# Moving gates, softmax factors and weight conversions to other places in an attention pipeline's pairs

## The chip, the cores and the metric

The kernel runs on one core of one Trainium2 chip. The metric is the device time of one execution in microseconds, lower is better. The kernel before has a median of 579.82 us over three runs (577.78 to 580.89). The core's engines are named as the profile names them: PE is TensorE (PEld its weight loads), DVE is VectorE, ACT is ScalarE, POOL is GpSimd, and SP issues most of the DMAs. Each of them works through its own queue in order.

## The reference

Three blocks follow one another on 4 batches of 448 positions.

```python
# 1. attention, 12 heads of 64
scores = cap * tanh(scale * q @ k.T / cap)
x = softmax(scores) @ v                     # heads side by side: 4 x 448 x 768
# 2. four attention experts of width 64, the best 2 of 4 per position
logits = x @ w_gate                         # rank them, softmax over the best two
for e in range(4):
    a = causal_softmax((x @ wq[e]) @ (x @ wk[e]).T / 8)
    out += gate[e] * (a @ (x @ wv[e]) @ wo[e])
# 3. gated MLP on that output
h = gelu(x @ w_in); u, v = split(h)
v = layer_norm(v) * g_ln
out = x + (u * (w_sg @ v + b_sg)) @ w_out
```

All tensors are float32. The two large weights `w_in` and `w_out` arrive as float64 and are turned into pairs of float32 parts on the chip.

## The kernel before

**The pairs.** `slot(n)` (line 252) is one step of the attention. There are 24 pairs of heads (4 batches with 6 pairs each), and slots 0 to 24. In slot n, PE makes the scores of pair n in two halves (`scores`, 191), ACT takes tanh and exp of them, and PE multiplies the weights of pair n - 1 with its values (`values`, 218). DVE and POOL sum the exponentials (POOL the first sum `pb`, DVE the next two in `add_up`, 213), and after every second pair PE folds these sums over the partitions (`sums`, 229) into `rs`.

**The places.** Between these steps `slot` calls `side(place)`, at which the second block and the weights' preparation are woven in. The places of a slot come in this order: "a" (called a0) in the first half of the scores, before their exp; "w" before the values product; "a" again (a1) after it; "p" after the second half of the scores; then sums and `add_up`; "n" last. Up to slot 9 `side` comes from `prepare_weights` (559), which converts `w_in`; from slot 10 on it comes from `beside` (522). PE, ACT, DVE and POOL keep the order of the program through slot 24 (`InOrder`, `pin`), so an instruction that waits holds everything behind it on its engine. After slot 24 a scheduler chooses the order (`pe_pin[0] = False`, 642).

**Normalising.** When batch b's pairs are done, `normed` (317) does the rest in steps: `invert` (241) takes the reciprocal of `rs`, writes it to DRAM (`rd`) and loads it back spread over partitions (`rb`, two tiles, tags rb0 and rb1, `load_rb`); `over_sums` multiplies (`os`); `in_parts` splits x into `xh` and `xl` for products in parts. A batch has three such thirds, 0 to 2. The steps stand at the second, fourth and fifth slot after its last pair.

**Experts.** `PLAN` (474) lists the second block of a batch by slots counted from the one in which its x is ready: queries and keys (`queries_keys`, 355), scores with their row minima (`weigh`, 416: a PE product into a PSUM tile `a`, on DVE the masked minimum `m`, on ACT the exp `pe`, which frees the PSUM tile), values and logits (`values_chunk`, 374), the gates (`gates`, 390: 13 small DVE instructions with one ACT exp among them), the factors and POOL's scaling (`settle`, 436: six small DVE instructions for `cs`, eight on POOL that scale `pe`), transposes (`turn`, 447: PE `tr`, DVE `pt`) and the product with the values (`attend`, 459). The PSUM tiles of `weigh`, `values_chunk`, `queries_keys`, `turn` and `sums` share one pool of three buffers (`ps_g`, 124). Slots n with n % 6 = 0 (12, 18, 24) have minima and two value chunks.

**w_out.** `w_out(k, i)` (338) converts one of eight pieces of the last weight: a DMA into `wuw`, six DVE instructions (`from64`, into `wum`), three on POOL, two DMAs to DRAM (`wud`). Its tiles take the tags rb0 and rb1. Six pieces run at place "w" of slots 11, 12, 17, 18, 23 and 24, loaded one slot earlier at "n"; the other two run in `experts_end` (546), which holds all of the experts' work behind slot 24.

**The end.** After slot 24, `experts_end` is interleaved with the MLP's parts (line 827), 0.35 units of the MLP for each unit of the experts. `mlp_weights(1)` (667, 685) waits until all eight pieces of w_out are done, then loads them as `wu_h` and `wu_l`, whose buffers are those of the query and key weights. `mlp_a(1)` takes the tags rb0 and rb1 for its own `yh` and `yl` (815).

Of the kernel before, what the change touches and what calls it, by code (L numbers as in the profile page):

```python
# [13 lines left out]
I32 = mybir.dt.int32  # L14
# [58 lines left out]
def build(ctx: ExitStack, tc: tile.TileContext, a: dict):  # L73
# [48 lines left out]
    wp = ES(tc.tile_pool(name="wp", bufs=2))  # L122
    dr = ES(tc.tile_pool(name="dr", bufs=2, space=bass.MemoryType.DRAM))
# [193 lines left out]
    def normed(n, place):  # L317

        b = (n - 1) // HP - 1
        step = (n % HP, place)  # L320
        if n > B * HP + 4 or b < 0:
            return
        if step == (1, "w"):
            invert(b)
        elif step == (3, "w"):
            over_sums(b, 0)
            over_sums(b, 1)
            load_rb(b, 2)
        elif step == (4, "w"):
            in_parts(b, 0)  # L330
            in_parts(b, 1)
            over_sums(b, 2)
        elif step == (4, "a1"):
            in_parts(b, 2)
# [3 lines left out]
    def w_out(k, i):  # L338

        o = slice(i * DM // 2, (i + 1) * DM // 2)  # L340
        w = xp.tile([128, DM], F32R, tag="rb0", name=f"wuw{k}_{i}")
        me = xp.tile([128, DM], I32, tag="rb1", name=f"wum{k}_{i}")
        hi, lo = w[:, :DM // 2], w[:, DM // 2:]
        nc.sync.dma_start(w.bitcast(I64), a["w_out"][:, k, o])
        yield WC
        p, e = from64(w, me[:, :DM // 2], me[:, DM // 2:])
        rnd("p", hi, p)
        pool_e.tensor_tensor(p, p, hi.bitcast(F32), op=ALU.subtract)
        pool_e.tensor_tensor(lo, p, e, op=ALU.add)
        for t in range(2):  # L350
            nc.sync.dma_start(wu_d[t][:, k, o], (hi, lo)[t].bitcast(F32))
        wu_done.append((k, i))
        yield 1.0
# [105 lines left out]
    def attend(b, ep):  # L459
# [7 lines left out]
        if ep == 0:  # L467
# [9 lines left out]
            3: [("a", weigh, 0, 2), ("a", weigh, 0, 3), ("p", values_chunk, 2), ("p", values_chunk, 3)],  # L477
            4: [("w", gates), ("w", settle, 0), ("p", queries_keys, 1, 0), ("t", turn, 0, 0)],
# [3 lines left out]
            8: [("w", settle, 1), ("t", turn, 1, 0)],  # L482
# [3 lines left out]
    def planned(n):  # L486

        work = {"a": [], "w": [], "p": [], "t": []}
        for b in reversed(range(B)):
            for place, f, *args in PLAN.get(n - (b + 1) * HP - 4, []):  # L490
                work[place].append((b, f, args))
        return work
# [27 lines left out]
    ws = [w_out(k, i) for k in range(4) for i in range(2)]  # L520

    def beside(n):
# [4 lines left out]
        def side(place):  # L527
            if place == "a":
                drain(run(work["a"][:1]))
                del work["a"][:1]  # L530
                normed(n, halves.pop(0))
            elif place == "p":
                drain(together(run(work["p"]), run(work["t"]), 0.3))
            elif place == "w":
                drain(run(work["w"]))
                normed(n, place)
                experts_weights(n, place)
                if n > HP + 4 and n % HP in (5, 0):
                    drain(ws.pop(0))
            else:  # L540
                experts_weights(n, place)
                if n > HP + 3 and n % HP in (4, 5):
                    next(ws[0])
        return side

    def experts_end(n):

        for m in range(n, B * HP + 20):
            work = planned(m)
            for place in "aw":  # L550
                yield from run(work[place])
            normed(m, "w")
            normed(m, "a1")
            yield from together(run(work["p"]), run(work["t"]), 0.3)
            if ws:
                yield from ws.pop(0)


    def prepare_weights(pool):
# [36 lines left out]
        def side(n):  # L596
            todo = list(turns[n])

            def at_place(place):
# [16 lines left out]
                if n > 0:  # L616
                    normed(n, place)
# [5 lines left out]
    xp = ES(tc.tile_pool(name="xp", bufs=1, reuse_waits="tile"))  # L623
# [202 lines left out]
    elif ORD == 3:  # L826
        drain(together(ex, mlp(((mlp_a, 0), (mlp_weights, 1), (mlp_b, 0), (mlp_a, 1), (mlp_c, 0), (mlp_b, 1), (mlp_a, 2))), LRATIO))
# [69 lines left out]
```

## Time and profile before

| | |
|---|---|
| median of 3 runs | 579.82 us (577.78 to 580.89) |
| the profiled execution, its own time | 579.84 us |
| span of the core in it | 578.1 us |
| PE busy | 536.1 us (93%) |
| DVE busy | 375.5 us (65%) |
| ACT busy | 324.5 us (56%) |
| POOL busy | 140.8 us (24%) |
| share of the chain of waits on PE / DVE / ACT / DMA | 60% / 19% / 8% / 6% |
| mean granted PE clock | 0.973 of full |

The profile's times are from the span's start. The execution's time is 1.74 us above the span. In the chain of waits one follows back from the last instruction what released what. The tables of stretches give for each stretch the busy time of each engine and, as PEclk, the clock that PE was granted: 1.00 is 2.4 GHz, 0.50 would be 1.2 GHz throughout. In timelines a bracket gives how long the engine sat idle before the row and what released it. All instructions that go through a helper have the line of the helper (L104, L119), so one goes by tile names.

### The profile page before, as it was taken

The page shows a single profiled execution, that of the slowest core. Times are in us where ns is not written, and L with a number is a line of the kernel's source. Part 1 is how long each engine was busy: PE and PEld are TensorE (multiplying, and loading weights), DVE is VectorE, ACT ScalarE, POOL GpSimd, SP SyncE. Part 2 cuts the span into 40 slices and gives each one's busy share as a digit, 9 for nine tenths or more (in the row PEclk, how much of TensorE's full clock was granted, in tenths as well). Part 3 has the DMA queues.
Part 4 walks back from the last instruction along what each step waited for, and adds up shares of the span by engine and source line. Part 5 has one row for each costly group of instructions (what it writes and reads, how often), then busy time and mean ns, then how long its engine had stood idle before and what let it go on. Part 6 is the DMA issues. An engine that isn't in the chain of part 4 may idle for free.

```text
span 578.1 us, 7562 instructions
## 1 busy us (share of the span) xinstructions
PE 536.1 (93%) x2732; PEld 350.7 (61%) x2732; DVE 375.5 (65%) x725; ACT 324.5 (56%) x508; POOL 140.8 (24%) x180
## 2 busy tenths in 40 slices
PE   7999999798879997999968995899999999999997
PEld 2333333445545556555535763777878888989996
DVE  3999999774666754666765654857861688475310
ACT  5988888576757784767742343462643444243211
POOL 0000131133141144141163145417512121031000
PEclk9999999899999997999998999899999998999999
DMA  8974425833412231411118313100511000101111
GB/s 243 330 228 128 163 76 156 248 104 108 114 62 80 76 119 61 124 53 49 28 55 236 100 56 75 42 14 1 182 70 65 1 1 27 38 16 49 49 48 64
DMA packets 30596, 53.97 MB, mean 93 GB/s; under 512 B 3872, under 2 KB 22880, under 8 KB 30560
## 3 DMA queue, kind: packets, MB, share of 16 engines
q1 hardware_dynamic: 29408, 48.26, 27.5%
q0 software_dynamic: 1152, 5.24, 2.7%
q8 instruction: 21, 0.34, 0.3%
q14 instruction: 15, 0.12, 0.1%
HBM read 41.83 MB, written 11.67 MB: 93 GB/s over the span
## 4 chain that ended last, share of the span: by engine, by line
PE 60%; DVE 19%; ACT 8%; DMA 6%; issue 4%; POOL 2%; SPq 0%; DVEq 0%; POOLq 0%; ACTq 0%
PE o L119 15%; PE sp L119 7%; PE s L119 6%; PE qk L119 6%; PE po L119 6%; ACT p L104 5%; PE v L119 4%; DVE pb L104 3%; PE tr L454 3%; PE hu L119 3%; PE a L119 2%; DVE rs L104 2%; PE hv L119 2%; DVE wum L104 2%; PE w2ps L119 2%
## 5 line engine op out<-in xcount | busy, mean ns | idle before, releaser
L104 ACT ACTIVATE p<-s,tsc 112x896 f32<-112x896 f32 x96 | 91.3, 1004 | 25.0 <-PE s L119 20.0
L104 POOL TENSOR_TENSOR pb<-p 112x896 f32<-112x896 f32 x18 | 39.8, 2214 | 219.1 <-ACT p L104 134.8
L119 PE MATMUL s<-qp,kp 64*112 64x448 f32 x384 | 84.4, 557 | 3.5 <-ACT p L104 3.5
L104 ACT ACTIVATE p<-p,capt 112x1792 f32<-112x1792 f32 x48 | 85.9, 1790 | 1.3
L119 PE MATMUL po<-p,vv 112*64 112x448 f32 x384 | 77.3, 545 | 0.0
L104 DVE TENSOR_TENSOR pb<-pb,p 112x896 f32<-112x896 f32 x48 | 54.7, 1140 | 13.0 <-ACT p L104 12.2
L119 PEld LDWEIGHTS s<-qp,kp 64*112 64x112 f32 x384 | 31.0, 173 | 51.1 <-issue 22.4
L104 ACT ACTIVATE pe<-a,m 112x112 f32<-112x112 f32 (+3 forms) x64 | 31.1, 491 | 43.6 <-DVE m L104 41.5
L119 PEld LDWEIGHTS po<-p,vv 112*64 112x64 f32 x384 | 25.5, 136 | 45.0 <-issue 43.3
L119 PE MATMUL qk<-xh,wqk_h 128*128 128x448 f32 x96 | 39.4, 411 | 9.7 <-DVE xh L104 8.7
L454 PE MATMUL tr<-ident,pe 112*112 112x112 f32 x160 | 26.2, 276 | 12.6 <-ACT pe L104 8.2
L104 POOL TENSOR_SCALAR pe<-pe,cs 112x112 f32<-112x112 f32 (+1 forms) x64 | 32.8, 533 | 20.0 <-DVE cs L104 19.9
L119 PE MATMUL qk<-xh,wqk_l 128*128 128x448 f32 x96 | 36.1, 376 | 0.0
L119 PE MATMUL o<-gl,wu_h 128*128 128x448 f32 x96 | 35.6, 371 | 0.0
L119 PE MATMUL o<-gh,wu_l 128*128 128x448 f32 x96 | 35.3, 370 | 0.0
L119 PE MATMUL o<-gh,wu_h 128*128 128x448 f32 x96 | 35.3, 368 | 0.0
L104 DVE CUSTOM_DVE_ANT_0 a<-a,neg 112x112 f32<-112x112 f32 (+3 forms) x64 | 27.7, 466 | 10.9 <-PE a L119 10.9
L119 PE MATMUL v<-wvg_h,xh 128*112 128x260 f32 x96 | 30.7, 319 | 4.3 <-ACT pe L104 4.3
L104 DVE COPY pt<-tr 112x112 f32<-112x112 f32 (+3 forms) x32 | 14.1, 449 | 27.0 <-PE tr L454 26.9
L119 PE MATMUL a<-qk 64*112 64x112 f32 (+3 forms) x128 | 27.6, 430 | 3.7 <-ACT pe L104 2.6
L119 PEld LDWEIGHTS qk<-xh,wqk_h 128*128 128x128 f32 x96 | 18.8, 196 | 19.8 <-DVE xh L104 9.8
L454 PEld LDWEIGHTS tr<-ident,pe 112*112 112x112 f32 x160 | 19.0, 139 | 18.2 <-POOL pe L104 10.0
(226 smaller groups left out, 1132.1 us busy)
## 6 DMA issues: line engine op xcount, KB each, us to landing
kp<-in_kT_dram SPq DMA_DIRECT2D x24, 224.0 KB, 4.5
qp<-in_qT_dram SPq DMA_DIRECT2D x24, 224.0 KB, 4.6
vv<-in_v_dram SPq DMA_DIRECT2D x24, 224.0 KB, 4.4
rb<-rd SPq DMA_DIRECT2D x24, 224.0 KB, 5.0
out_dram<-ob SPq DMA_DIRECT2D x24, 224.0 KB, 1.9
wuw<-in_w_out_dram SPq DMA_DIRECT2D x8, 384.0 KB, 3.3
wud<-wuw SPq DMA_DIRECT2D x16, 192.0 KB, 1.8
ws<-in_wqk_dram SPq DMA_DIRECT2D x4, 384.0 KB, 5.8
```

Source lines behind the costliest of these rows:

```text
L104: ins = f(*args, **kw)
L119: pin(nc.tensor.matmul(*args, **kw))
L454: pin(nc.tensor.transpose(g[:CP, j * CP:(j + 1) * CP], pe[:, j * CP:(j + 1) * CP], ident))
```

## The change

Pieces of work change their places; none is added or taken away. In the pairs: the gates go from "w" of the fifth slot of a plan to "n" of the fourth; `settle` goes from "w" to a0 (a new list "s"), behind the minima of that place; the reciprocal of the sums goes from "w" to a1, behind the minima; the split of x for batches 1 to 3 has one third at "w" and two at a1 (before: two and one), and batch 0 has its first two thirds split in slot 9, the tenth pair, and the last at "w" of slot 10. In slots with n % 6 = 0 the first value chunk runs without transposes between. The conversions of w_out run at slots 11, 14, 17, 20 and 23 and, for the last three pieces, at steps 29 to 31 of `experts_end`; four of them take the tag ws. The pool `xp` is opened earlier in the program. In the MLP's order `mlp_b(0)` comes ahead of `mlp_weights(1)`.

```diff
-        if step == (1, "w"):
+        if step == (1, "a1"):
             invert(b)
         elif step == (3, "w"):
             over_sums(b, 0)
             over_sums(b, 1)
             load_rb(b, 2)
-        elif step == (4, "w"):
+        elif b == 0 and step == (3, "a1"):
             in_parts(b, 0)
             in_parts(b, 1)
+        elif step == (4, "w"):
+            if b:
+                in_parts(b, 0)
             over_sums(b, 2)
-        elif step == (4, "a1"):
+            if not b:
+                in_parts(b, 2)
+        elif b and step == (4, "a1"):
+            in_parts(b, 1)
             in_parts(b, 2)
...
-            3: [..., ("p", values_chunk, 2), ("p", values_chunk, 3)],
-            4: [("w", gates), ("w", settle, 0), ("p", queries_keys, 1, 0), ("t", turn, 0, 0)],
+            3: [..., ("p", values_chunk, 2), ("p", values_chunk, 3), ("n", gates)],
+            4: [("s", settle, 0), ("p", queries_keys, 1, 0), ("t", turn, 0, 0)],
...
-            8: [("w", settle, 1), ("t", turn, 1, 0)],
+            8: [("s", settle, 1), ("t", turn, 1, 0)],
...
-    ws = [w_out(k, i) for k in range(4) for i in range(2)]
+    W_OUT = {11: ("w", xp, "rb0", "rb1"), 14: ("n", at, "ws", "ws"), 17: ("w", at, "ws", "ws"),
+             20: ("n", at, "ws", "ws"), 23: ("w", at, "ws", "ws"),
+             29: ("n", xp, "rb0", "rb1"), 30: ("n", xp, "rb0", "rb1"), 31: ("n", xp, "rb0", "rb1")}
+    ws = {n: w_out(*divmod(u, 2), *W_OUT[n][1:]) for u, n in enumerate(W_OUT)}
...
             if place == "a":
                 drain(run(work["a"][:1]))
                 del work["a"][:1]
-                normed(n, halves.pop(0))
+                half = halves.pop(0)
+                drain(run(work.pop("s", [])))
+                normed(n, half)
             elif place == "p":
-                drain(together(run(work["p"]), run(work["t"]), 0.3))
-            elif place == "w":
-                drain(run(work["w"]))
+                first = work["p"][:1] if n % HP == 0 else []
+                drain(run(first))
+                drain(together(run(work["p"][len(first):]), run(work["t"]), 0.3))
+            else:
+                drain(run(work[place]))
                 normed(n, place)
                 experts_weights(n, place)
-                if n > HP + 4 and n % HP in (5, 0):
-                    drain(ws.pop(0))
-            else:
-                experts_weights(n, place)
-                if n > HP + 3 and n % HP in (4, 5):
-                    next(ws[0])
+                if n in W_OUT and W_OUT[n][0] == place:
+                    drain(ws[n])
+                if place == "n" and n + 1 in W_OUT:
+                    next(ws[n + 1])
...
-        drain(together(ex, mlp(((mlp_a, 0), (mlp_weights, 1), (mlp_b, 0), (mlp_a, 1), ...
+        drain(together(ex, mlp(((mlp_a, 0), (mlp_b, 0), (mlp_weights, 1), (mlp_a, 1), ...
```

## Rows read from the trace of the kernel before

**Rows 1.** The page: the span, and busy time of PE with its share.

```profile
span 578.1 us, 7562 instructions
PE 536.1 (93%) x2732; PEld 350.7 (61%) x2732; DVE 375.5 (65%) x725; ACT 324.5 (56%) x508; POOL 140.8 (24%) x180
```

**Rows 2.** Stretches, slots 10, 12, 13, 14, 18, 24: length, busy PE PEld DVE ACT POOL, PEclk.

```profile
99.34:117.01 17.67, 14.38 (x60) 7.02 (x59) 12.92 (x13) 10.35 (x11) 2.76 (x1) 0.82 0.77 230
...
127.52:142.02 14.50, 12.75 (x86) 7.59 (x85) 7.77 (x17) 9.64 (x17) 5.93 (x5) 1.00 0.44 140
142.02:156.28 14.26, 12.65 (x81) 7.51 (x77) 10.47 (x15) 10.22 (x18) 2.10 (x1) 1.00 0.23 71
156.28:171.94 15.66, 12.71 (x69) 6.59 (x68) 8.83 (x26) 10.70 (x13) 5.91 (x9) 1.00 0.36 104
...
208.77:229.27 20.50, 16.55 (x95) 11.16 (x95) 11.30 (x28) 10.99 (x19) 9.27 (x12) 0.83 0.33 105
...
295.23:312.14 16.91, 12.76 (x79) 8.95 (x79) 9.70 (x28) 3.06 (x11) 8.24 (x13) 0.80 0.42 120
...
340.00:370.00 30.00, 21.59 (x102) 15.45 (x100) 18.66 (x47) 10.84 (x30) 13.93 (x19) 0.89 0.24 56
```

**Rows 3.** Waits of PE: us in total, times, longest.

```profile
PE qk L119 <- DVE xh L104: 8.7, 3, 5.4
PE tr L454 <- ACT pe L104: 8.2, 3, 4.1
PE v L119 <- ACT pe L104: 4.3, 3, 1.7
```

**Rows 4.** Timeline of DVE in slot 18: start, us, instruction.

```profile
214.07 0.36 DVE L104 TENSOR_SCALAR wum<-wuw 128x384 int32<-128x384 int32 x1 [1.12 <-DMA wuw<-in_w_out_dram]
...
219.26 0.39 DVE L104 CUSTOM_DVE_ANT_0 a<-a,neg 112x224 f32<-112x224 f32 x1
```

**Rows 5.** Timeline of POOL in slot 18.

```profile
216.42 4.71 POOL L104 TENSOR_SCALAR pe<-pe,cs 112x112 f32<-112x112 f32 x8
```

**Rows 6.** Timeline of DVE in slot 15: the first copies of the transposes.

```profile
179.29 0.58 DVE L104 COPY pt<-tr 112x112 f32<-112x112 f32 x2 [2.43 <-PE tr L454]
```

**Rows 7.** Timeline of DVE in slot 14: `pb` of pair 13, then the gates.

```profile
158.77 2.21 DVE L104 TENSOR_TENSOR pb<-pb,p 112x896 f32<-112x896 f32 x2
...
162.13 0.17 DVE L104 TENSOR_TENSOR wt<-lg,gmx 112x16 f32<-112x16 f32 x1
```

**Rows 8.** Timeline of ACT in slot 14.

```profile
158.55 1.91 ACT L104 ACTIVATE p<-s,tsc 112x896 f32<-112x896 f32 x2
160.48 1.79 ACT L104 ACTIVATE p<-p,capt 112x1792 f32<-112x1792 f32 x1
```

**Rows 9.** Timeline of PE in slot 14: the second half of the scores.

```profile
161.13 1.76 PE L119 MATMUL s<-qp,kp 64*112 64x448 f32 x8
```

**Rows 10.** Timeline of DVE in slots 9 and 10.

```profile
101.42 2.20 DVE L104 TENSOR_TENSOR pb<-pb,p 112x896 f32<-112x896 f32 x2
...
109.77 0.96 DVE L104 TENSOR_TENSOR wvg_l<-ws,wvg_h 128x780 fp32r<-128x780 f32 x1
110.65 0.62 DVE L104 CAST xh<-os 128x896 fp32r<-128x896 f32 x1
```

**Rows 11.** Timeline of DVE in slot 16, beside a `pb` of POOL.

```profile
189.10 2.98 DVE L104 TENSOR_TENSOR os<-os,rb 128x896 f32<-128x896 f32 x1
```

**Rows 12.** Timeline of SP behind slot 24.

```profile
326.65 0.35 SPq L344 DMA_DIRECT2D wuw<-in_w_out_dram  x1
...
343.40 0.33 SPq L344 DMA_DIRECT2D wuw<-in_w_out_dram  x1
350.42 2.47 SPq L351 DMA_DIRECT2D wud<-wuw  x2
354.55 1.24 SPq L301 DMA_DIRECT2D rb<-rd  x2
```

**Rows 13.** Chain of waits, start and us: first products of `mlp_a(1)`.

```profile
404.69 2.79 PE hv L119 x12
```

More of the change, by code (lines that the diff above doesn't have):

```diff
@@ L122, in build @@
     wp = ES(tc.tile_pool(name="wp", bufs=2))
+    xp = ES(tc.tile_pool(name="xp", bufs=1, reuse_waits="tile"))
     dr = ES(tc.tile_pool(name="dr", bufs=2, space=bass.MemoryType.DRAM))
@@ L328, in normed, with w_out @@
             load_rb(b, 2)
-        elif step == (4, "w"):
+        elif b == 0 and step == (3, "a1"):
             in_parts(b, 0)
             in_parts(b, 1)
+        elif step == (4, "w"):
+            if b:
+                in_parts(b, 0)
             over_sums(b, 2)
-        elif step == (4, "a1"):
+            if not b:
+                in_parts(b, 2)
+        elif b and step == (4, "a1"):
+            in_parts(b, 1)
             in_parts(b, 2)
     wu_done = []
-    def w_out(k, i):
+    def w_out(k, i, pool, *tags):
         o = slice(i * DM // 2, (i + 1) * DM // 2)
-        w = xp.tile([128, DM], F32R, tag="rb0", name=f"wuw{k}_{i}")
-        me = xp.tile([128, DM], I32, tag="rb1", name=f"wum{k}_{i}")
+        w = pool.tile([128, DM], F32R, tag=tags[0], name=f"wuw{k}_{i}")
+        me = pool.tile([128, DM], I32, tag=tags[1], name=f"wum{k}_{i}")
         hi, lo = w[:, :DM // 2], w[:, DM // 2:]
@@ L476, in build @@
             2: [("a", weigh, 0, 0), ("a", weigh, 0, 1), ("p", values_chunk, 0), ("p", values_chunk, 1)],
-            3: [("a", weigh, 0, 2), ("a", weigh, 0, 3), ("p", values_chunk, 2), ("p", values_chunk, 3)],
-            4: [("w", gates), ("w", settle, 0), ("p", queries_keys, 1, 0), ("t", turn, 0, 0)],
+            3: [("a", weigh, 0, 2), ("a", weigh, 0, 3), ("p", values_chunk, 2), ("p", values_chunk, 3), ("n", gates)],
+            4: [("s", settle, 0), ("p", queries_keys, 1, 0), ("t", turn, 0, 0)],
             5: [("p", queries_keys, 1, 1), ("t", turn, 0, 1)],
@@ L486, in planned @@
     def planned(n):
-        work = {"a": [], "w": [], "p": [], "t": []}
+        work = {"a": [], "s": [], "w": [], "p": [], "t": [], "n": []}
         for b in reversed(range(B)):
@@ L549, in experts_end @@
             work = planned(m)
-            for place in "aw":
+            for place in "asw":
                 yield from run(work[place])
-            normed(m, "w")
-            normed(m, "a1")
+            for place in ("w", "a1"):
+                normed(m, place)
             yield from together(run(work["p"]), run(work["t"]), 0.3)
-            if ws:
-                yield from ws.pop(0)
+            yield from run(work["n"])
+            normed(m, "n")
+            if m in W_OUT:
+                yield from ws[m]
     def prepare_weights(pool):
@@ L596, in side @@
         def side(n):
-            todo = list(turns[n])
+            todo, halves = list(turns[n]), ["a0", "a1"]
             def at_place(place):
@@ L616, in at_place @@
                 if n > 0:
-                    normed(n, place)
+                    normed(n, halves.pop(0) if place == "a" else place)
             return at_place
@@ L621, in build @@
     PRE_SLOTS = HP + 4
-    xp = ES(tc.tile_pool(name="xp", bufs=1, reuse_waits="tile"))
     with tc.tile_pool(name="pre", bufs=2) as pre:
@@ L826, in build @@
     elif ORD == 3:
-        drain(together(ex, mlp(((mlp_a, 0), (mlp_weights, 1), (mlp_b, 0), (mlp_a, 1), (mlp_c, 0), (mlp_b, 1), (mlp_a, 2))), LRATIO))
+        drain(together(ex, mlp(((mlp_a, 0), (mlp_b, 0), (mlp_weights, 1), (mlp_a, 1), (mlp_c, 0), (mlp_b, 1), (mlp_a, 2))), LRATIO))
         drain(together(mlp_c(1), mlp(((mlp_b, 2), (mlp_a, 3))), L1 * 18600. / C))
```

## The prediction

> **What bounds the kernel now.** I read the page first: PE is busy 536.1 of 578.1 us [rows 1], so no change of places can save more than the other 42 us, plus what PE loses while its clock is low. DVE, the next, has 65%. So the question is where PE stands still, and the table of stretches by slot answers it [rows 2]. A stretch loses its length less PE's busy time, and its length times what PEclk lacks to 1.00, since at the lower level (1.2 instead of 2.4 GHz) a matmul takes twice as long. That gives: slot 10, 17.67 - 14.38 = 3.3 idle and 0.18 x 17.67 = 3.2 by the clock, 6.5 in all; slot 12, 1.75; slot 13, 1.6; slot 14, 2.95; slot 18, 3.95 + 0.17 x 20.5 = 7.4; slot 24, 4.15 + 0.20 x 16.91 = 7.5; and 340 to 370, 8.4 + 0.11 x 30 = 11.7. Together 39 us. The other slots show 0.9 at most and are not touched below unless said.
>
> The waits of PE say for what it stood still [rows 3]. "tr <- ACT pe" (8.2, slots 18 and 24) and "v <- ACT pe" (4.3) are no data that PE reads: the product needs a PSUM buffer, and the three are held by scores whose minimum DVE has not taken. DVE's timeline of slot 18 shows why [rows 4]. Behind the first minima stands a piece of w_out; it first waits for its DMA, starts at 214.07, and the second minimum runs at 219.26, 5.2 us later. In slot 13 the reciprocal stands in the same place. Slot 14 waits for the factors `cs`, slot 10 and 340 to 370 for `xh` ("qk <- DVE xh", 8.7 with one of 5.4).
>
> **The change part by part.** The sum is made against the profiled execution, 579.84 us with 1.74 of it outside the span; the median, 579.82, is the same.
>
> *w_out out of slots 12, 18 and 24.* The minima then follow PE at once and free the buffers. Slot 12 gives back 1.75. Slot 18 gives back 7.4, its low clock included, for the clock fell behind that wait; but the first value chunk now runs alone, and the transposes after it take its buffer, which ACT empties behind an exp of 1.79 [rows 8]. I take 1.0 for that (0 to 1.8): 6.4. In slot 24 there are no scores, so ACT is free; 7.5 less 0.5 for short waits: 7.0.
>
> *w_out into "n" of slots 14 and 20.* Six instructions on DVE: those that took 5.2 us from 214.07 on, beside work of POOL [rows 4]; part of that is contention. Then come three on POOL. Queued behind on DVE are two `over_sums` and the copies of the transposes, which PE needs in slots 15 and 21; on POOL the next `pb`, which has the slot's rest; on SP two stores, and the next loads behind them, which are wanted a slot later. DVE now stands idle 2.43 ahead of these copies [rows 6]. So 5.2 - 2.4 = 2.8 could stick out in each slot, or nothing; I take 0.3 each, near the low end, as POOL has no `pb` to run at that point: -0.6. Slots 17 and 23 keep their pieces at "w" and cost nothing new, and each load goes out one slot early, as before.
>
> *The reciprocal behind the minima.* Slot 13 gives 1.6. Its DMAs (one store, four loads) go out some 3 us later; `over_sums` uses them two slots later, so nothing waits. In slot 7 it moves behind a conversion, some 4 us later, and the use is in slot 9: that cover is thin, and if it failed it would be part of slot 10 below.
>
> *Gates at the end of the fourth slot, factors at a0.* On DVE nothing overtakes: `pb` at 158.77, gates behind it, already the same order. The gain is that the factors no longer meet POOL's `pb`, and POOL scales before its `pb`, not after. POOL's eight scalings (4.71 us, [rows 5]) now stand ahead of `pb`, which only DVE's `add_up` at the end of the slot needs: covered. But a wait is added on ACT. The exp of the gates now stands ahead of the next slot's first tanh; before, ACT went on with that tanh at 158.55 [rows 8], while the exp's input comes at 162.13 + 0.17 [rows 7]. ACT stands 3.7 us, and both tanh, exp and PE's second scores queue behind it. PE reaches these 161.13 - 156.28 = 4.85 us into the slot [rows 2, 9]; the first tanh (about 0.95, half of 1.91) would end some 5.5 us into it. So 0.7 sticks out in slot 14 (0 to 3.7); in slot 20 `attend` lies between and covers it. Slot 14: 2.95 - 0.7 = 2.25.
>
> *x of batch 0 split in slot 9.* Two thirds are now split ahead of `pb` of pair 9 (2.20, [rows 10]), so that this `pb` falls on the time of POOL's own. First the row: an `os` beside POOL's `pb` took 2.98 [rows 11], and a DVE `pb` of the same size 1.1 (half of 2.20), so DVE's `pb` will wait about 1.9 us. The last third, for which PE waits longest, saves only the place of `wvg_l` (0.9: 109.77 to 110.65, [rows 10]). I take 0.9, between 0 and the 6.5 that slot 10 loses, near the low end by that row. For batches 1 to 3 the minimum now precedes two thirds, which are ready about when PE wants them: 0.
>
> *Behind slot 24.* Before, the last two pieces of w_out took rb0 and rb1 ahead of the load of batch 3's last third: that load is issued at 354.55, after the second piece's stores [rows 12], and PE waits 5.4 for it [rows 3]. Now the load comes first and the pieces after it. Of the 11.7 us lost between 340 and 370 I take 6.0: the wait and its low clock make up 5.4 + 3.3 = 8.7, but a third piece of w_out is added here (one piece spans 343.40 to 352.89, [rows 12]) and other waits lie close. Bounds: 0 and 11.7. The new order of `mlp_b(0)` moves it ahead of a wait in the program and costs nothing while the last pieces are in time.
>
> Sum: 0.9 + 1.75 + 1.6 + 2.25 - 0.6 + 6.4 + 7.0 + 6.0 = 25.3. 579.84 - 25.3 = **554.5 us**.
>
> One rule speaks against the new places. By the Trainium skill, page "SBUF — State Buffer", section "Who interferes with whom", a DVE instruction with two SBUF inputs and a GpSimd instruction that reads SBUF contend, and the later one blocks fully. Rows 11 bear it out for a `pb`; no row shows it for w_out's three POOL instructions beside `over_sums`. By it the new pieces in slots 14 and 20 would stick out by the full 2.8 us each, and the sum would be 559.5; that is the third rival.
>
> **The rivals.**
> 1. *The time behind slot 24 stays*: another wait takes the place of `xh`, as in each of the several short waits there. For it: PE is idle 8.4 of 30 us there and only 5.4 of that is this wait. Time 554.5 + 6.0 = 560.5.
> 2. *All the waits go*, slot 10 and the end too: 554.5 - 5.6 - 5.7 = 543.2. Against it: DVE's queue in slot 10, above.
> 3. *DVE blocked by POOL* in slots 15 and 21, at the upper bound: 554.5 + 2 x (2.8 - 0.3) = 559.5. For it: [rows 4, 11]. Against it: POOL is 24% busy [rows 1].
> 4. *The wait moves to ACT*: the gates' exp sticks out by its full 3.7 in slots 14 and 20, the buffer of the first value chunk by 1.8, the low clock stays in slots 18 and 24 (3.5 + 3.4), and the end gains nothing: 554.5 + 3.0 + 3.7 + 0.8 + 6.9 + 6.0 = 574.9.
> 5. *Slower*: the last three pieces of w_out hold up PE. They run one after the other on one pair of tiles, twice 16.75 us from load to load (326.65 to 343.40) and 9.5 for the last [rows 12], 43 in all, and `wu_h` and `mlp_a(1)` wait for the third. Starting where the second of them starts now, at 343.40, they would be done at 386.4, against 404.69 for the first products of `mlp_a(1)` [rows 13]: 18 us of slack, 12 if the end gets 6 faster. It decides from the point where the pieces start 12 us later than that. Were they left to the end of the experts' work, some 43 - 12 = 31 us would be bare: 554.5 + 31 = 585.5.
> 6. *The change does nothing to what bounds it*, since pieces still stand ahead of minima in slots 17 and 23: 579.8. Against it: these slots show no loss now.
>
> **How the numbers follow.** Forecast 0.47; rival 1, 0.17; rival 2, 0.12; rival 3, 0.10; rival 4, 0.05; rival 5, 0.06; rival 6, 0.03. A measurement of this kernel can tell about 0.5% from no change, 2.9 us. Faster: 0.47 + 0.17 + 0.12 + 0.10 + 0.05 = 0.91; the same 0.03; slower 0.06. The range reaches down to rival 2 (543) and up to 569: rivals 1 and 3 together are at 565.5, and a third of the way from there to rival 4 is added; half of rival 4 and rivals 5 and 6 are left out.
>
> **What would show it.** Right: slots 12, 13, 18 and 24 within 1 us of their busy PE, PEclk 1.00 in 18 and 24, second minima within 1 us of PE's scores; a hole on ACT of 3 to 4 us ahead of the gates' exp; in slot 10 still a wait for `xh` of 2 us or more and a clock under 1.00; the last `rb` load some 20 us nearer to the end of slot 24. Wrong: a new wait of PE of over 2 us for `pt`, for `p` or for `wu_h`, or an end behind slot 24 that is longer than its 266 us now (312.14 to 578.1, [rows 1, 2]).

## The result, and the profile of the changed kernel

The kernel after the change takes 559.4 us (median of 4 runs, 557.46 to 559.89) against 579.82 us (four runs by now, 577.78 to 580.89): a ratio of 0.9646 with a 95% interval of 0.961 to 0.9681. The forecast was 554.5 us in a range of 543 to 569. The profiled execution took 559.72 us. The page's span and busy times, against [rows 1]:

```profile
span 558.0 us, 7562 instructions
PE 532.7 (95%) x2732; PEld 346.3 (62%) x2732; DVE 361.4 (65%) x725; ACT 325.7 (58%) x508; POOL 141.4 (25%) x180
```

PE's waits, against [rows 3] (us in total, times, longest):

```profile
PE s L119 <- ACT p L104: 3.4, 4, 1.7
PE a L119 <- ACT pe L104: 3.4, 3, 2.2
PE qk L119 <- DVE xh L104: 2.6, 1, 2.6
PE a L119 <- ACT qk L104: 2.1, 2, 1.3
PE tr L461 <- DVE lg L104: 1.8, 2, 1.5
...
PE tr L461 <- DVE pt L104: 1.1, 1, 1.1
```

"tr <- ACT pe" (8.2) and "v <- ACT pe" (4.3) are gone as leaders, "qk <- DVE xh" fell from 8.7 to 2.6. "a <- ACT pe" (2.6 before) and "a <- ACT qk" (0.9 before) grew; new are "tr <- DVE lg" and, small, "tr <- DVE pt". The table of stretches shows where the time came from: slots 10, 12, 13, 14, 18, 19 and 24, then three stretches behind slot 24 (length, busy PE PEld DVE ACT POOL, PEclk, DMA share, GB/s), as in [rows 2].

```profile
98.25:112.40 14.15, 11.56 (x60) 5.71 (x59) 12.80 (x13) 9.86 (x11) 2.09 (x1) 1.00 0.78 226
122.77:135.26 12.49, 12.49 (x85) 7.54 (x84) 4.68 (x13) 11.46 (x20) 3.43 (x2) 1.00 0.45 140
135.26:147.63 12.37, 12.37 (x81) 7.41 (x77) 8.55 (x13) 10.66 (x17) 2.09 (x1) 1.00 0.24 75
147.63:160.56 12.93, 12.51 (x70) 6.56 (x69) 7.04 (x26) 8.80 (x11) 5.94 (x9) 1.00 0.43 125
...
197.43:212.61 15.18, 13.65 (x95) 8.48 (x94) 6.20 (x22) 10.89 (x19) 5.92 (x9) 1.00 0.36 116
212.61:227.45 14.84, 13.70 (x91) 8.32 (x87) 9.36 (x17) 10.49 (x16) 2.09 (x1) 1.00 0.23 74
...
279.41:290.37 10.96, 10.66 (x79) 7.07 (x79) 5.81 (x22) 3.06 (x11) 5.06 (x10) 1.00 0.50 148
290.37:320.00 29.63, 26.42 (x143) 19.11 (x140) 19.47 (x51) 8.59 (x21) 6.71 (x13) 1.00 0.45 118
320.00:350.00 30.00, 26.03 (x103) 17.45 (x103) 27.43 (x63) 15.63 (x39) 16.27 (x19) 0.77 0.18 54
350.00:558.00 208.00, 201.07 (x1019) 172.09 (x1017) 107.68 (x231) 77.98 (x171) 45.66 (x77) 0.99 0.14 48
```

The kernel before, in three stretches from the end of its slot 24:

```profile
312.14:342.14 30.00, 27.48 (x154) 20.51 (x151) 19.60 (x51) 8.53 (x21) 9.25 (x15) 1.00 0.39 115
342.14:372.14 30.00, 21.00 (x101) 14.73 (x100) 20.37 (x55) 12.89 (x38) 13.12 (x18) 0.89 0.27 63
372.14:578.10 205.96, 199.72 (x1011) 171.38 (x1010) 111.38 (x234) 80.32 (x173) 43.44 (x71) 0.99 0.13 46
```

Through slot 24 the change gains 312.14 - 290.37 = 21.8 us, and in each of the slots shown PEclk is now 1.00. Behind slot 24 it gains nothing: 265.96 us before, 267.63 after. There the second stretch changed its nature. Before, PE stood 9.0 of 30 us at a clock of 0.89. Now it stands only 4.0, but the clock is 0.77 and DVE is busy 27.43 of 30. What the idle time gave, the clock took back in this execution. Four kernels of the experiments below run the same program behind slot 24 (x0_back, x0_recip_back, recip_18, no_first). In their first 60 us behind it they lose, by length times what PEclk lacks to 1.00, 5.1 to 6.6 us, the kernel after 6.9, the kernel before 3.3, and their stretch takes 264.9 to 266.6. So the clock took back a part in each of them and the end gained at most 1 us. DVE's timeline of the changed kernel in that stretch:

```profile
308.93 1.09 DVE L104 TENSOR_TENSOR os<-os,rb 128x896 f32<-128x896 f32 x1 [2.38 <-DMA rb<-rd]
...
321.65 2.40 DVE L104 CAST xh<-os 128x896 fp32r<-128x896 f32 x3 [5.49 <-PE qk L119]
323.97 3.08 DVE L104 TENSOR_TENSOR xl<-os,xh 128x896 fp32r<-128x896 f32 x3
326.98 0.27 DVE L104 CUSTOM_DVE_ANT_0 a<-a,neg 112x112 f32<-112x112 f32 x1
...
327.76 0.53 DVE L104 TENSOR_SCALAR wum<-wuw 128x384 int32<-128x384 int32 x1
```

The last load of `rb` is no longer late: the third `os` is done at 310. But `xh` and `xl` of batch 3 have the tiles of batch 2's x, which PE still reads; DVE stands 5.49 us for PE's last `qk` on them, then splits all three thirds in one go (5.3 us), and the minima come behind that, with a w_out piece between the next ones. PE's side of it:

```profile
324.34 1.33 PE L119 MATMUL a<-qk 64*112 64x112 f32 x6
327.90 1.08 PE L119 MATMUL a<-qk 64*112 64x224 f32 x2 [2.23 <-ACT pe L104]
...
341.53 1.00 PE L119 MATMUL a<-qk 64*112 64x448 f32 x2 [1.27 <-ACT qk L104]
...
343.44 0.57 PE L119 MATMUL sp<-sg_l,vh 112*128 112x448 f32 x1
```

With each of these two waits the granted clock falls to its lower level (1.2 GHz): 0.50 from 328 to 332 and from 343.4 to 350, some 7 us each time. A product with 448 columns, as the last row, then takes 0.57 instead of 0.37 us.

### The profile page after: what moved, and what is told of

Its sections match the earlier page's. It is cut to its first block, busy times and chain, and to the rows that moved or that the text cites. A ratio compares the mean times of both kernels' runs of the same rounds, so it can differ in the third digit from the quotient of the medians.

```text
span 558.0 us, 7562 instructions
## 1 busy us (share of the span) xinstructions
PE 532.7 (95%) x2732; PEld 346.3 (62%) x2732; DVE 361.4 (65%) x725; ACT 325.7 (58%) x508; POOL 141.4 (25%) x180
## 4 chain that ended last, share of the span: by engine, by line
PE 73%; DVE 16%; ACT 6%; DMA 2%; issue 2%; POOL 1%; DVEq 0%; POOLq 0%; ACTq 0%; SPq 0%
PE o L119 15%; PE po L119 10%; PE s L119 10%; PE qk L119 8%; PE sp L119 7%; PE v L119 5%; ACT p L104 4%; PE a L119 3%; PE hv L119 3%; PE hu L119 3%; PE w2ps L119 2%; PE tr L461 2%; PE av L119 2%; DVE pb L104 2%; DVE rs L104 2%
## 5 line engine op out<-in xcount | busy, mean ns | idle before, releaser
L104 DVE TENSOR_TENSOR pb<-pb,p 112x896 f32<-112x896 f32 x48 | 57.3, 1194 | 16.0 <-ACT p L104 12.3
L104 POOL TENSOR_SCALAR pe<-pe,cs 112x112 f32<-112x112 f32 (+1 forms) x64 | 31.6, 519 | 50.3 <-DVE cs L104 50.2
L119 PE MATMUL qk<-xh,wqk_h 128*128 128x448 f32 x96 | 38.2, 398 | 2.6 <-DVE xh L104 2.6
L119 PE MATMUL a<-qk 64*112 64x112 f32 (+3 forms) x128 | 29.9, 440 | 5.6 <-ACT pe L104 3.4
L104 ACT ACTIVATE ob<-o 128x448 f32<-128x448 f32 x24 | 13.0, 541 | 31.5 <-PE o L119 31.3
L119 PE MATMUL v<-wvg_h,xh 128*112 128x260 f32 x96 | 28.7, 299 | 0.7 <-ACT pe L104 0.7
L461 PE MATMUL tr<-ident,pe 112*112 112x112 f32 x160 | 23.7, 261 | 4.9 <-DVE lg L104 1.8
L119 PE MATMUL v<-wvg_h,xl 128*112 128x260 f32 x96 | 27.1, 283 | 0.0
L119 PE MATMUL v<-wvg_l,xh 128*112 128x260 f32 x96 | 27.1, 282 | 0.0
```

The lines of the kernel that those rows point to most:

```text
L104: ins = f(*args, **kw)
L119: pin(nc.tensor.matmul(*args, **kw))
L461: pin(nc.tensor.transpose(g[:CP, j * CP:(j + 1) * CP], pe[:, j * CP:(j + 1) * CP], ident))
```

## The experiments

Theory A is the forecast's terms slot by slot, with a jam behind slot 24 that has two halves: the tiles of x, and the three w_out pieces on a full DVE. The rivals stand in each expectation. The slots' lengths below are read from PE's timeline of each profiled run, from a slot's first scores to the next one's (slot 24, which has no scores, from its first product to the end of its sums); "behind" runs from the end of slot 24's sums to the end of the span. This way of reading puts slot 24 at 16.98 and 11.03.

| run | slot 10 | 12 | 14 | 18 | 19 | 20 | 24 | behind | median us | ratio to before (95%) |
|---|---|---|---|---|---|---|---|---|---|---|
| before | 17.67 | 14.50 | 15.66 | 20.50 | 13.72 | 14.48 | 16.98 | 265.9 | 579.82 | |
| after | 14.15 | 12.49 | 12.93 | 15.18 | 14.84 | 14.17 | 11.03 | 267.6 | 559.4 | 0.9646 (0.961 to 0.9681) |
| wout_back | 14.14 | 14.48 | 13.37 | 21.82 | 14.83 | 14.17 | 15.02 | 268.4 | 575.01 | 0.9941 (0.9916 to 0.9966) |
| gates_back | 14.14 | 12.49 | 14.49 | 15.19 | 14.85 | 14.49 | 11.02 | 266.8 | 561.24 | 0.969 (0.9644 to 0.9736) |
| x0_back | 15.11 | 12.49 | 12.93 | 15.18 | 14.86 | 14.19 | 11.02 | 266.6 | 560.9 | 0.9698 (0.965 to 0.9745) |
| x0_recip_back | 16.47 | 12.49 | 12.92 | 15.19 | 14.83 | 14.17 | 11.00 | 264.9 | 561.76 | 0.9702 (0.9639 to 0.9765) |
| no_first | 14.13 | 12.49 | 12.93 | 13.47 | 14.82 | 14.17 | 11.82 | 265.1 | 558.29 | 0.9638 (0.9602 to 0.9675) |
| recip_18 | 14.14 | 12.49 | 12.94 | 15.18 | 15.85 | 14.17 | 11.03 | 266.4 | 558.88 | 0.9653 (0.9614 to 0.9692) |
| no_conv | 14.13 | 12.49 | 12.94 | 15.19 | 14.84 | 14.17 | 11.02 | 264.3 | 556.41 | 0.9607 (0.9552 to 0.9663) |
| qk_early | 14.15 | 12.49 | 12.94 | 15.18 | 14.85 | 14.19 | 11.03 | 264.6 | 557.28 | 0.9629 (0.9567 to 0.9692) |
| early_no_conv | 14.14 | 12.49 | 12.93 | 15.18 | 14.83 | 14.17 | 11.02 | 260.2 | 554.47 | 0.9568 (0.9544 to 0.9593) |
| order_back | 14.15 | 12.49 | 12.93 | 15.18 | 14.83 | 14.17 | 11.02 | 268.2 | 560.11 | 0.9671 (0.9647 to 0.9694) |
| piece_24 | 14.14 | 12.49 | 12.93 | 15.18 | 14.84 | 14.17 | 11.03 | 270.5 | 563.69 | 0.9732 (0.9689 to 0.9776) |
| combined | 14.16 | 12.49 | 12.93 | 13.47 | 13.70 | 14.17 | 11.02 | 272.3 | 565.58 | 0.9762 (0.9733 to 0.9791) |

The slots repeat to 0.04 us from run to run where nothing in them is changed; the stretch behind slot 24 does not, even where no edit of the run touches it (264.9 to 267.6 in after, x0_back, x0_recip_back, recip_18 and no_first; the gates of gates_back stand behind slot 24 too). So edits in slots are read from slots, and those behind slot 24 are only believed where they leave this range and the intervals of the ratios do not overlap.

**w_out at the places of before.**

```diff
+    W_OUT = {n: ("w" if n < 25 else "n", xp, "rb0", "rb1") for n in (11, 12, 17, 18, 23, 24, 25, 26)}
```

> The kernel after, but with the eight pieces of w_out at the places and in the tiles of before (slots 11, 12, 17, 18, 23, 24, two behind slot 24). Theory A, the forecast's own terms: minima again stand behind a piece, so slot 12 goes from 12.5 to 14.5 us, slot 18 from 15.2 to between 18.5 and 20.5, slot 24 from 11.0 to 16.9, with a clock under 1.00 in 18 and 24; the stretch behind slot 24 goes from 267.6 to about 266, as before the change, since the two pieces block the last load of rb again. Sum 570 us. Rival B: in slot 18 the first value chunk without transposes made the gain, and the factors at a0: slot 18 stays under 16.5 and the total is under 567. Rival C: with the last load of rb blocked again the stretch behind slot 24 gets longer, over 270, total over 573: then the new order of the MLP's parts had hidden a gain there.

Slots 12, 18 and 24 lost 2.0, 6.6 and 4.0 us, slot 14 another 0.4, and the median rose by 15.6: Theory A in kind, and rival B is out. The sizes were off: slot 18 took more than the 20.5 that Theory A allowed, slot 24 less than its 16.9, and the total is 5 above its 570. The stretch behind rose by 0.8 only, within its scatter, and stays under the 270 of rival C, whose total (over 573) came all the same, from the slots. The waits of PE in slot 18:

```profile
211.40 0.38 PE L119 MATMUL v<-wvg_h,xh 128*112 128x260 f32 x1 [2.25 <-ACT pe L104]
216.00 0.59 PE L461 MATMUL tr<-ident,pe 112*112 112x112 f32 x2 [3.80 <-DVE lg L104]
```

The second is the wait for the first chunk's buffer, 1.53 us in the kernel after and 3.80 here (the copy of `lg`, the buffer's last reader, waits for ACT). The kernel before stood there 3.93 us for `pe` instead, and its slot 18 was shorter (20.50).

**Gates and factors at the places of before.**

```diff
-            3: [..., ("n", gates)], 4: [("s", settle, 0), ...], 8: [("s", settle, 1), ...]
+            3: [...], 4: [("w", gates), ("w", settle, 0), ...], 8: [("w", settle, 1), ...]
```

> The kernel after, with the gates at w of the fifth slot and the factors at w, as before. Theory A: they alone made slot 14's gain: it goes from 12.9 back to 15.7, slot 20 from 14.2 to 14.5, total 562.5 to 563, and the hole of 3.7 us on ACT ahead of the gates' exp goes. Rival B: slot 14 also gained from minima that come earlier in slot 13: it comes back to 14.5 at most, total under 561.5. Rival C: the forecast's loss on ACT in slot 14 (0.7) was in truth larger, and with the gates back slot 18 or 24 loses too, since settle then stands behind attend: total over 564.

Slot 14 came back by 1.56 us, not by 2.73, slot 20 by 0.32: rival B. The rest of slot 14's gain belongs to other edits (0.44 of it came with w_out's places in the run above; 0.7 was not separated).

**The split of batch 0's x, then the reciprocal too.** The second run adds to the first that batch 0's reciprocal goes back to "w" of slot 7.

```diff
-        elif b == 0 and step == (3, "a1"):
-            in_parts(b, 0)
-            in_parts(b, 1)
         elif step == (4, "w"):
-            if b:
-                in_parts(b, 0)
+            in_parts(b, 0)
+            if not b:
+                in_parts(b, 1)
             over_sums(b, 2)
-            if not b:
-                in_parts(b, 2)
-        elif b and step == (4, "a1"):
-            in_parts(b, 1)
+        elif step == (4, "a1"):
+            if b:
+                in_parts(b, 1)
             in_parts(b, 2)
...
-        if step == (1, "a1"):
+        if step == (1, "a1" if b else "w"):
             invert(b)
```

> The kernel after, with the split of x at the places of before (batch 0 in slot 10, and for batches 1 to 3 two thirds at w and one at a1). Theory A: the split of batch 0 in slot 9 is what shortened slot 10: it goes from 14.15 back to 17 or more, with a clock under 0.9, slot 9 gets up to 1 us shorter, total 562 to 563. Rival B: the gain of slots 0 to 10 came from the reciprocal in slot 7: slot 10 stays under 15.5, total under 561.3. Slots 16 and 22 change by less than 0.3 in either case.

> The kernel after with the split of x as before (as in the run x0_back) and batch 0's reciprocal back at w of slot 7. In x0_back PE stood in slot 10 for the same two waits as in the kernel before (0.83 and 2.47 us), but its clock stayed at 1.00 where it had fallen to 0.69 and 0.50, and slot 10 took 15.1 instead of 17.7. Theory A: what PE does ahead of slot 10 decides it, and that is the reciprocal's place: with it back the wait of 0.65 ahead of slot 9 is there again, the clock falls again behind the same 2.47, slot 10 takes 17.0 to 17.7 and slot 9 starts 0.5 to 1 us later; total 563 to 564.5. Rival B: the reciprocal has no part in it: slot 10 stays at 15.1 with a clock of 1.00, total 560 to 562.

The kernels that ran moved batch 0's split only; batches 1 to 3 kept one third at w and two at a1, unlike what the text on record says. In x0_back slot 10 gave back 0.96 of its 3.52 us: rival B of the first, by its numbers (under 15.5 and under 561.3). PE of x0_back, slot 10:

```profile
107.28 0.47 PE L119 MATMUL qk<-xh,wqk_h 128*128 128x448 f32 x1 [0.83 <-DVE xh L104]
...
110.83 0.47 PE L119 MATMUL qk<-xh,wqk_h 128*128 128x448 f32 x1 [2.47 <-DVE xh L104]
111.13 0.37 PE L119 MATMUL qk<-xh,wqk_l 128*128 128x448 f32 x1
```

PE of x0_recip_back, the end of slot 8 and slot 10:

```profile
87.91 0.95 PE L119 MATMUL sum<-pb,onehot 112*32 112x448 f32 x4 [0.59 <-DVE pb L104]
...
110.95 0.74 PE L119 MATMUL qk<-xh,wqk_h 128*128 128x448 f32 x1 [2.47 <-DVE xh L104]
111.49 0.58 PE L119 MATMUL qk<-xh,wqk_l 128*128 128x448 f32 x1
```

The same wait of 2.47 us left the clock at the upper level in the first and was followed by the lower one in the second. Slot 10 took 16.47, the wait of 0.59 ahead of slot 9 was back: Theory A in kind, though short of the 17.0 to 17.7 that it named (before, the clock stayed low to the end of the slot, here to 114). Its other numbers did not come: slot 9 started 0.13 us later than in x0_back, not 0.5 to 1, and the median of two runs (561.76) is in rival B's range. Of the three kernels with these two waits in slot 10, the clock fell in the two with the reciprocal at "w" (before, x0_recip_back) and not in the one with it at a1, each profiled once; why a wait of 0.6 us some 20 us earlier should decide it is not shown. Chance is a rival: the executions of one kernel differ in the clock with nothing changed (the four of no_conv have means from 0.988 to 0.997 and times from 558.4 to 552.47). What is sure is the split's part: in all eleven kernels that split in slot 9, slot 10 has one wait and took 14.13 to 14.16.

**The first value chunk without transposes.**

```diff
-                first = work["p"][:1] if n % HP == 0 else []
+                first = []
```

> The kernel after, with transposes between the products of the first value chunk again in slots 18 and 24 (slot 12 has none). Theory A: the wait of 1.53 us in slot 18 is the price of the first chunk that runs alone (its PSUM buffer is emptied by ACT behind an exp): without it slot 18 falls from 15.18 to 14.2 or less, slot 24 stays within 0.4 of 11.0; total 558.5. Rival B: the chunk alone covers POOL's scalings, for which the transposes would wait: slot 18 gets longer, 16 or more, slot 24 too, 11.5 or more, total over 561.

In slot 18 running the chunk alone costs 1.71 us, the wait of 1.53 and its surroundings, more than the 1.0 that the forecast took and within its 0 to 1.8. In slot 24 it saves 0.79, where PE waits 0.78 for `pe` without it. Theory A for slot 18 and the total, rival B for slot 24 (11.82, over its 11.5). In the total the two medians are 1.1 us apart with overlapping intervals.

**Batch 2's reciprocal at the end of slot 18.**

```diff
+        if n == 3 * HP and place == "n":
+            invert(2)
...
+        if b == 2 and step == (1, "a1"):
+            return
```

> The kernel after, with batch 2's reciprocal at the end of slot 18 (n) instead of at a1 of slot 19, where it now stands ahead of the copies of the transposes. Theory A: slot 19 falls from 14.84 to 13.7, as before the change, since DVE has the time at the turn of the slots; total 558.3. Rival B: it now stands ahead of slot 19's first minima and PE waits for pe: slot 19 stays over 14.4, total 559 to 561.

A miss: slot 19 got 1.0 us longer, not 1.1 shorter. The reciprocal (2.95 from 215.99) now stands ahead of the first minima (218.85), as in rival B, though the median (558.88) is just under rival B's 559. In the run "combined" it is at "w" of slot 19, its place before, and the slot takes 13.70. So of three places "w" costs nothing, a1 1.1 us and the turn of the slots 2.1.

**The two halves of the jam behind slot 24.** no_conv leaves out the conversion of the last three pieces; qk_early puts batch 2's last queries and keys one step earlier; early_no_conv does both.

```diff
-        p, e = from64(w, me[:, :DM // 2], me[:, DM // 2:])
...
+                if not (b == 2 and f is queries_keys and args[0] == 1):
+                    work[place].append((b, f, args))
+            if b == 2 and i in (3, 4):
+                work["p"].append((b, queries_keys, (1, i - 3)))
```

> The kernel after, with the conversion of the last three pieces of w_out left out: their DMAs in and out stay (the words come from another input of the same size), the six instructions on DVE and three on POOL of each are gone, so these columns of the second MLP weight are not computed. Theory A: behind slot 24 DVE is full between 325 and 350, and these 18 instructions on DVE (some 12 us with contention) are what holds back the minima, PE and its clock: the stretch behind slot 24 falls from 267.6 to 261 or less, total 553 or less. Rival B: the split of batch 3's x waits until PE has read batch 2's x out of the same tiles (DVE stands 5.5 us for it until 321.65) and then holds the minima for 5.5 us; the conversions fill gaps: the stretch stays within 1.5 us of 267.6, the wait of PE for pe near 328 stays over 1.5 us, total 558 to 560.

> The kernel after, with the queries and keys of batch 2's second pair of experts one step of the plan earlier (at the end of slots' numbers 25 and 26, not 26 and 27). They are the last products that read batch 2's x, whose tiles batch 3's x takes. Theory A: the jam behind slot 24 has two halves, and this is the first: DVE's wait of 5.49 us for these products goes or falls under 2, the split of x (5.5 us of DVE) comes some 5 us earlier and no longer stands ahead of the minima at 327, PE's wait of 2.23 for pe falls under 1 and the clock between 320 and 340 (0.81, 0.85) is over 0.95; the stretch behind slot 24 falls from 267.6 to 264.5 or less, total 556.5. Rival B: transposes that have no other products beside them now wait for their copies, or the w_out pieces jam DVE as before: the stretch stays within 1 us of 267.6, total 558.5 to 560.

> The runs qk_early and no_conv together: batch 2's last queries and keys one step earlier, and the conversion of the last three pieces of w_out left out (these columns of the second MLP weight are not computed). Theory A: two jams add up behind slot 24, the wait for the tiles of x and the conversions: each alone gave some 3 us, together 5 to 7; without the first piece POOL's scaling is not held up, PE's wait of 3.2 for it goes; the stretch behind slot 24 is 260.5 to 262.5, the clock over 0.95 from 310 to 350, total 552 to 554. Rival B: both runs gained the same time (the clock's), and together they give no more than one: the stretch stays at 263.5 to 265, total 555.5 to 557.5.

The stretch behind slot 24 fell by 3.2, 3.0 and 7.3 us, the medians by 3.0, 2.1 and 4.9. Against the five kernels that leave the stretch alone (264.9 to 267.6) neither of the first two is clear: 264.3 and 264.6 lie 0.6 and 0.3 below the lowest, and the intervals of their ratios overlap with that of the kernel after. The third is clear of both: 260.2, and 0.9544 to 0.9593 against 0.961 to 0.9681. So the two halves together are shown to cost some 5 to 7 us, and each half's own share is not. no_conv lies between its two theories; qk_early falls just short of the stretch that Theory A named, and its clock between 320 and 340 is 0.74, not over 0.95. In the third, rival B (both gained the same time, 263.5 to 265) is out, and Theory A holds to within 0.5 us, with the clock at 0.94 where it named over 0.95. Windows 320 to 350 and 350 to 380 of no_conv:

```profile
320.00:350.00 30.00, 27.18 (x118) 18.65 (x117) 24.05 (x58) 15.94 (x40) 11.59 (x15) 0.89 0.16 49
350.00:380.00 30.00, 29.16 (x176) 23.08 (x176) 17.82 (x49) 14.78 (x40) 8.10 (x15) 1.00 0.09 27
```

and of early_no_conv:

```profile
320.00:350.00 30.00, 26.72 (x124) 19.21 (x123) 23.87 (x56) 17.01 (x43) 15.15 (x21) 0.94 0.14 47
```

The clock went from 0.77 to 0.89 to 0.94: of the two falls of the kernel after, the first, behind a wait of 1.56, stays, and the second is gone. That the pieces made just this second fall is not shown, for recip_18, which keeps all three, does not have it either:

```profile
330.00:340.00 10.00, 8.80 (x34) 5.70 (x35) 9.79 (x24) 4.52 (x14) 8.64 (x9) 0.66 0.14 42
340.00:350.00 10.00, 9.34 (x39) 6.21 (x38) 9.30 (x25) 6.18 (x16) 4.03 (x7) 1.00 0.19 62
```

Nor have x0_back, x0_recip_back and no_first. These four fall between 316 and 326 instead, behind a wait of PE for POOL's scalings of 1.35 to 2.45 us (0.68 in the kernel after), and once more between 326 and 339. What holds is the count: from the end of slot 24 to 380 the clock falls two or three times in the five kernels that leave the stretch alone, and once in no_conv, qk_early and early_no_conv each. In qk_early the split comes at 317.25 instead of 321.65, as wanted, but POOL shows why only a part is gained:

```profile
317.27 5.05 POOL L104 TENSOR_SCALAR wuw<-wum 128x384 fp32r<-128x384 f32 x1 [4.02 <-DVE cs L104]
322.30 3.81 POOL L104 TENSOR_SCALAR pe<-pe,cs 112x112 f32<-112x112 f32 x8
```

The same instruction in the kernel after:

```profile
316.10 0.51 POOL L104 TENSOR_SCALAR wuw<-wum 128x384 fp32r<-128x384 f32 x1 [4.07 <-DVE cs L104]
```

One POOL instruction of a w_out piece took 5.05 us, as long as DVE's six instructions of the split ran (317.25 to 321.95), and the eight scalings were queued behind it: PE waited 3.20 for `pe`, where the five kernels wait 0.68 to 2.45. By the Trainium skill, page "SBUF — State Buffer", section "Who interferes with whom", casts of DVE and its instructions with two SBUF inputs can hold POOL off altogether, and the order of issue decides who waits. The trace agrees, and adds that here POOL did not come in between one instruction of DVE and the next. In early_no_conv it did: the eight scalings had started before the split, took 6.88 us beside it, and DVE's six took 5.7 instead of 4.8.

**The order of the MLP's parts as before.**

```diff
-        drain(together(ex, mlp(((mlp_a, 0), (mlp_b, 0), (mlp_weights, 1), (mlp_a, 1), ...
+        drain(together(ex, mlp(((mlp_a, 0), (mlp_weights, 1), (mlp_b, 0), (mlp_a, 1), ...
```

> The kernel after with the order of the MLP's parts as before: the loads of the last weights and their wait for w_out ahead of mlp_b(0). Theory A: mlp_b(0)'s products now fill PE between 338 and 360, where the experts' small products wait for DVE; held up until the last piece is done (358) they are missing there, and the stretch behind slot 24 gets 5 us longer or more, total over 564. Rival B, the forecast's: the order costs nothing while the pieces are in time; the stretch stays within 1.5 us of 267, total 558 to 561.

Rival B, the forecast's own: 0.6 us in the stretch and 0.7 in the median, inside the scatter.

**A piece at the end of slot 24, alone and combined.**

```diff
-             20: ("n", at, "ws", "ws"), 23: ("w", at, "ws", "ws"),
-             29: ("n", xp, "rb0", "rb1"), 30: ("n", xp, "rb0", "rb1"), 31: ("n", xp, "rb0", "rb1")}
+             20: ("n", at, "ws", "ws"), 23: ("w", xp, "rb0", "rb1"), 24: ("n", at, "ws", "ws"),
+             30: ("n", xp, "rb0", "rb1"), 31: ("n", xp, "rb0", "rb1")}
```

> The kernel after with the first of the last three pieces of w_out at the end of slot 24 and nothing else changed (slot 23's piece takes rb0 and rb1). Theory A: with a third of the conversions out of the jam the stretch behind slot 24 gains about a third of no_conv's 3 us or a little more, 265.5 to 266.5, total 558; slots 23 and 24 stay at 12.6 and 11.0. Rival B: the piece stands ahead of batch 3's reciprocal on DVE and its stores ahead of the loads of rb, the x of batch 3 comes 3 us later or more and the stretch gets longer than 268.5, total over 560.5.

> The kernel after with what the runs so far favour: the first value chunk alone in slot 24 only (transposes between in 18), batch 2's reciprocal at w of slot 19, batch 2's last queries and keys one step earlier, and the first of the three last w_out pieces at the end of slot 24 instead of among them (slot 23's piece then takes rb0 and rb1). Theory A: the terms add: slot 18 13.5 (-1.7), slot 19 13.7 (-1.1), slot 24 11.0, the stretch behind slot 24 263 to 265 (-3 to -5, as POOL's scaling no longer stands behind a piece that DVE's split of x holds up); total 551.5 to 554. Rival B: the stretch behind slot 24 keeps its 266 to 268, as whatever is taken out of the jam is given back by the clock there: total 556 to 557. Rival C: the piece in slot 24 delays the reciprocal or the loads of rb of batch 3, and the split of x with them: the stretch gets longer than 268, total over 557.5.

Both lost: the stretch took 270.5 and 272.3 us, Theory A fell in both, and rival B of piece_24 and rival C of combined have the result. In combined the slots did as expected (18: 13.47, 19: 13.70, together -2.9 us), and it is the slower kernel all the same. The mechanism is not quite the one that was written. The table of piece_24 for its first 20 us behind slot 24, then its waits of PE:

```profile
290.00:310.00 20.00, 14.25 (x64) 10.87 (x62) 11.77 (x29) 3.32 (x10) 4.80 (x7) 0.66 0.61 179
```

```profile
296.02 0.56 PE L119 MATMUL v<-wvg_h,xh 128*112 128x260 f32 x1 [2.49 <-ACT pe L104]
303.68 1.53 PE L461 MATMUL tr<-ident,pe 112*112 112x112 f32 x7 [2.85 <-DVE lg L104]
```

and DVE of piece_24, where the MLP's first input is split:

```profile
313.33 1.09 DVE L104 TENSOR_TENSOR os<-os,rb 128x896 f32<-128x896 f32 x1 [7.05 <-DMA rb<-rd]
314.34 0.62 DVE L104 CAST yh<-y 128x896 fp32r<-128x896 f32 x1
```

The last `rb` landed later (`os` at 313.33 instead of 308.93), as rival B says. More than that, `yh` of batch 0 came at 314.34 where the kernel after has it at 291.04 (combined: 311.46), so the MLP's products, which filled PE between 293 and 310, were missing. In the rows `yh` stands directly behind the `os` for which DVE waited 7.05 us, and the loads of the MLP's first weight, which its products need too, were issued at 301.02, behind POOL's part of the piece (298.41 to 301.08), where the kernel after issues them at 286.05. Two causes are open. One is the order of the queues alone. The other is space: the MLP's tiles take that of the pools that close behind slot 24, and a piece there keeps its tile until its store, issued at 304.69. No run tried it with another tile.

## Why the forecast was right, and where it was not

The time came out 4.9 us above the forecast and inside its range: the loop gave 21.8 us where 19.3 were forecast, the end gave nothing where 6.0 were. That is the time of rival 1 (560.5), whose sentence was that another wait takes the place of `xh`. That the loop gave more than forecast is in good part luck: the clock in slot 10 and slots 0 to 9 gave 3.7 us that no term had (2.6 and 1.1), and they cover shortfalls of 1.1 in slot 18, 1.0 in slot 24 and 1.1 in slot 19. Of the forecast's own signs of being wrong one came, an end longer than 266 us (267.6, within the scatter of that stretch), and two signs of being right did not: slot 18 is 1.5 us over its busy PE, and the clock in slot 10 is 1.00.

- *w_out out of 12, 18, 24*: right in kind. 2.0, 5.3 and 6.0 against 1.75, 6.4 and 7.0. In slot 18 the reserve for the first chunk's buffer was too small: 1.0 was taken, the runs show 1.7. In slot 24 wout_back takes back only 4.0 of the 6.0; 0.8 comes with the first chunk (no_first) and 1.2 is not separated. The clock stayed at 1.00 in 18 and 24, as forecast.
- *w_out into "n" of 14 and 20*: 0.3 each was charged, and slots 15 and 21 took 11.44 us where they had taken 11.41 and 11.42. Rival 3 did not come. The six DVE instructions, priced at 5.2 us, took 2.7 in slot 15, as POOL was idle beside them. The two `os` behind them met POOL's part: they took 2.40 us (2.09 before, without it), and POOL's first two conversions 1.28 and 1.73 (0.52 and 1.01 in slot 23), so there it was mostly POOL that waited.
- *Reciprocal behind the minima*: slot 13 gave 1.9 (forecast 1.6). The step "nothing waits" failed in slot 19, where transposes follow: the reciprocal stands ahead of their copies, PE waits 1.05, and the slot lost 1.1.
- *Gates and factors*: slot 14 gave 2.7 (2.25), ACT's hole ahead of the gates' exp is 3.68 us long as forecast, and it sticks out on PE by 0.42 (0.7 was taken). By gates_back only 1.6 of the 2.7 is this edit's.
- *x of batch 0*: mis-sized, 3.5 instead of 0.9. 0.96 came back in x0_back. The other 2.6 is the clock, which I had expected under 1.00; 1.4 of it came back with the reciprocal in slot 7, whose only price in the forecast was a thin cover. With one profile of each kernel the clock's part cannot be split between the two edits and chance.
- *Behind slot 24*: the step that failed. "The wait and its low clock make up 5.4 + 3.3" was right for the wait: it is gone, and the last load of `rb` comes 13 us behind slot 24 instead of 42. But the next thing late was not named: the tiles of batch 2's x, freed by PE at 321.65, and the three pieces on a DVE that is then busy 27.43 of 30 us. Both taken away, the stretch falls by 7.3 us (early_no_conv). The 5 us of idle time that PE got back went into a clock of 0.77 in the profiled execution.
- *The order of mlp_b(0)*: nothing was forecast, and nothing is seen.
- *Slots 0 to 9*: nothing was forecast and 1.1 us came. Slot 9 started at 89.17 before and between 87.85 and 88.79 in the other kernels; the wait of 0.65 ahead of it goes with the reciprocal's place in slot 7, but x0_recip_back has it too (0.59) and started at 88.79, so most of the 1.1 us is not explained.

What stays open: 0.7 us of slot 14, 1.2 of slot 24, what each half of the jam costs by itself, what makes the clock fall in slot 10, and whether the combined edits without the piece in slot 24 would beat the kernel after. qk_early and no_first have lower medians (557.28 and 558.29) but intervals that overlap with it; early_no_conv computes less. No run shows a complete kernel that is faster beyond doubt.

## What to carry to other kernels

When a wait is taken away by having its data earlier, ask for each operand when its destination is free too: here the load came 29 us earlier, counted from the end of slot 24, and the tiles that its data go into were still being read 11 us after the data were there. Put long instructions of an in-order engine where nothing short that another engine waits for follows in that slot, and check every slot in which the moved step recurs, since one of three may hold transposes. Edits of the same size can be told apart by slots to 0.04 us, while a stretch that a scheduler fills scatters by 2 to 3 us and needs a difference beyond that. The same holds for the clock: where a single profile shows a fall that another lacks, look at kernels that run the same program there before the fall is given a cause.

## What the runs showed of the hardware that was not expected

- A wait of 2.47 us of PE, on the same products, left the granted clock at 1.00 in x0_back and was followed by the lower level in x0_recip_back and before; one of 2.59 in the kernel after left it at 1.00. The length of the one wait does not settle it. Behind slot 24, too, the same wait of 0.73 (on `a`) was followed by the lower level in no_first and left 1.00 in the kernel after.
- POOL's 5.05 us for an instruction that takes 0.51 elsewhere, beside six instructions of DVE back to back. In early_no_conv, too, the eight scalings took 6.88 us beside the split, against 3.84 in the kernel after, but there the two engines took turns.
- Less idle time of PE need not be less time: in the profiles before and after, behind slot 24 PE's idle time fell by 3.7 us (17.8 to 14.1) and its busy time rose by 5.3 (248.2 to 253.5) for the same products.
